# Unit 8's q and k transposed by DMA, with the kernel's whole list of work laid out anew

## The chip, the cores and the metric

The kernel runs on one core of one Trainium2 chip. A core has five engines that work from queues of their own: TensorE (in the profile PE for matmuls and PEld for weight loads), VectorE (DVE), ScalarE (ACT), GpSimd (POOL) and SyncE (SP, which here only issues transfers). Transfers run on 16 DMA engines; SyncE, ScalarE and GpSimd can issue them. The metric is the time of one execution on the device in microseconds. Before the change it is 204.08 us, the median of 3 runs (201.86 to 205.74).

## The reference, cut to what matters

Two computations follow each other: a linear attention with a decaying state, in blocks of 64 positions, for 4 batches of 8 heads, and a two-layer network with a leaky activation on its output, taken as 3072 rows of 512.

```python
B, H, S, D = 4, 8, 768, 64
for b in range(S // 64):                       # blocks of 64 positions
    qb, kb, vb = q[:, :, sl], k[:, :, sl], v[:, :, sl]
    intra = einsum('bhic,bhjc->bhij', qb, kb) * Dmask     # lam ** (i - j), 0 above the diagonal
    intra = einsum('bhij,bhjd->bhid', intra, vb)
    inter = einsum('bhid,bhde->bhie', qb * lam_pow, kv_state)
    out[:, :, sl] = intra + inter
    kv_state = lam_block * kv_state + einsum('bhsd,bhse->bhde', kb * rev_pow, vb)

x = out.transpose(0, 2, 1, 3).reshape(3072, 512)
h = x @ w_in                                   # 512 -> 2048
g = maximum(h, 0) + alpha * minimum(h, 0)
y = g @ w_out                                  # 2048 -> 512
```

## The kernel before

The attention goes by 24 units. A unit is 256 positions (two blocks of 128) of one batch and four heads: unit n is `(c, bi, hh)`, with c the chunk of the network's rows (0 to 5), bi one of its two batches and hh the half of the heads. Four units make a chunk of 512 rows, which the network then takes.

For a unit these steps are called, each a function with the unit's number:

- `load` brings q or k as float32 (tiles `qraw`, `kraw`, pools of five buffers), through SyncE's queue or, with "G", GpSimd's; `load_v16` brings v as float16 through GpSimd's.
- `cast` makes float16 of q or k into one tile `qk16`; `key_decayed` makes `kdec`, k times its decay.
- q and k must stand with the head's 64 columns on the partitions (`qkT`). Units 0 to 8 get that from TensorE: `turn` issues four 128x128 transposes for each of q and k into a PSUM bank `tp` (L316), and `turn_copy` brings them to SBUF on VectorE or ScalarE. Units 9 to 23 get it from one DMA, `turned`, on SyncE's queue (L303).
- `decayed` makes `qdT`, q times its decay. `score_products` (L377), `masked` (on VectorE, L388: `sm`), `inter` (L361) and `intra` (L402) make the output in PSUM tile `acc`, and `attended` copies it into `xT`, the network's input.
- `state_products` (L422) adds to the state in PSUM, in the other half of `acc`; `first_state` (ScalarE, L449) and `states` (VectorE, L457) bring it to `R`, which the `inter` of a later block reads. In units 4 to 7 the first block has no state before it, so `inter(n)` reads what `first_state(n)` of the same unit wrote.

The network's first layer is `up(c, f)`: four matmuls of 512 columns into a PSUM bank (L498), then `relu` on ScalarE (m, L511) and `prelu` on VectorE (g, L520). Its second layer is `down` for chunk 0 (L528, with `down_copy` and `down_store`); for chunks 1 to 5 it is `second` (L632), and the first layer of chunks 4 and 5 together is `first` (L757). These two use a scheme with seven products of half-size blocks in place of eight, which needs sums of the operands beforehand: `w_sum` of w_out, `in_sum` of w_in, `g_sum` of g and `x_sum` of xT. Each of them is one instruction on VectorE or, with "G", on GpSimd (L550 and L553).

Nothing schedules at run time. The order is a list of 1043 calls at the end of the kernel, written out by hand or by a tool, and each engine's queue holds its instructions in the order in which the calls stand there. An instruction that waits holds up all that is behind it on its engine. The engine of a step is an argument of its call ("A" ScalarE, "V" VectorE, "G" GpSimd, "P" VectorE from PSUM). PSUM banks come from a pool of four. `tick` and `fill` are matmuls whose results nobody reads, in the opening. `gate(2, "out")` is a transfer of one number of w_out on SyncE's queue: SyncE can issue none of the later loads before the third quarter of w_out has landed.

Of the kernel before, what the change touches and what calls it, by code (L numbers as in the profile page):

```python
# [11 lines left out]
def kernel(  # L12
# [16 lines left out]
    nc = tc.nc  # L29
# [452 lines left out]
    G = {}  # L482
# [299 lines left out]
    mask_logs(0)  # L782
    key_decay()
    state_decay()
    load(0, 0, "k", None)
    cast(0, "k16", "V")
    query_decay(0, 1)
    load(0, 0, "q", None)
    key_decayed(0, "V")
    mask_logs(1)  # L790
    key_decayed(1, "V")
    decay_mask(2)
    decay_mask(0)
    cast(1, "k16", "V")
    tick(56)
    load(0, 1, "q", 1, "G")
    load_v16(1)
    decay_mask(1)
    cast(1, "q16", "A")
    mask_logs(3)  # L800
    query_decay(1, 1)
    cast(0, "q16", "V")
    turn(1, (1,))
    turn_copy(1, (1,), "V")
    decay_mask(3)
    query_decay(0, 0)
    load_alpha()
    load(0, 1, "k", 1, "G")
    load_v16(0)
    turn(1, (0,))  # L810
    turn_copy(1, (0,), "V")
    load_v16(2)
    turn(0, (1,))
    turn_copy(0, (1,), "V")
    turn(0, (0,))
    turn_copy(0, (0,), "A")
    load_v16(3)
    load_win(1)
    slopes_turn()
    slopes()  # L820
    load_win(0)
    decayed(1, "P")
    cast(2, "q16", "A")
    score_products(1)
    masked(1)
    fill(3)
    key_decayed(2)
    cast(2, "k16", "A")
    cast(3, "q16", "G")
    turn(2, (0,))  # L830
    turn_copy(2, (0,), "V")
    state_in(1, 0)
    first_state(1)
    decayed(2)
    cast(3, "k16", "A")
    decayed(0)
    score_products(0)
    masked(0)
    turn(2, (1,))
    turn_copy(2, (1,), "A")  # L840
    key_decayed(3)
    inter(1)
    intra(1)
    attended(1, "A")
    load_win(3)
    turn(3, (0,))
    turn_copy(3, (0,), "A")
    state_in(0, 0)
    first_state(0)
    load(1, 0, "q", 0, "G")  # L850
    score_products(2)
    masked(2)
    turn(3, (1,))
    turn_copy(3, (1,), "A")
    state_in(2, 0)
    first_state(2)
    decayed(3)
    load(1, 0, "k", 0, "G")
    load(1, 0, "q", 1, "G")
    load_win(2)  # L860
    inter(0)
    intra(0)
    attended(0, "A")
    load_v16(4)
    load(1, 0, "k", 1, "G")
    state_in(1, 1)
    states(1, (1,))
    load_wout(0)
    score_products(3)
    masked(3)  # L870
    state_in(3, 0)
    first_state(3)
    inter(2)
    intra(2)
    attended(2, "A")
    load(1, 1, "q", 1, "G")
    state_in(2, 1)
    states(2, (1,))
    state_in(3, 1)
    states(3, (1,))  # L880
    state_in(0, 1)
    states(0, (1,))
    cast(4, "q16", "G")
    inter(3)
    intra(3)
    attended(3, "A")
    up(0, 4, 0)
    relu(0, 4, 0)
    up(0, 5)
    up(0, 3)  # L890
    up(0, 6)
    prelu(0, 4, 0)
    relu(0, 5)
    relu(0, 3)
    prelu(0, 5)
    up(0, 7)
    relu(0, 6)
    up(0, 13)
    prelu(0, 3)
    up(0, 15)  # L900
    relu(0, 7)
    prelu(0, 6)
    relu(0, 13)
    turn(4, (0,))
    relu(0, 15)
    prelu(0, 7)
    up(0, 14)
    load(1, 1, "k", 1, "G")
    prelu(0, 13)
    turn_copy(4, (0,), "A")  # L910
    up(0, 1)
    relu(0, 14)
    prelu(0, 15)
    cast(4, "k16", "G")
    turn(4, (1,))
    load_v16(5)
    load_wout(1)
    up(0, 0)
    prelu(0, 14)
    cast(5, "q16", "A")  # L920
    up(0, 4, 1)
    turn_copy(4, (1,), "A")
    relu(0, 1)
    relu(0, 4, 1)
    cast(5, "k16", "G")
    load(1, 1, "q", 0, "G")
    up(0, 9)
    key_decayed(4, "V")
    state_products(4, None, True)
    in_sum(1, 1, "G")  # L930
    score_products(4)
    load_wout(2)
    prelu(0, 1)
    prelu(0, 4, 1)
    relu(0, 0)
    relu(0, 9)
    turn(5, (0,))
    cast(7, "q16", "G")
    up(0, 12)
    relu(0, 12)  # L940
    first_state(4)
    load_wout(3)
    prelu(0, 0)
    w_sum(1, 1, "G")
    decayed(4)
    up(0, 2)
    turn_copy(5, (0,), "V")
    relu(0, 2)
    turn(5, (1,))
    prelu(0, 9)  # L950
    up(0, 11)
    relu(0, 11)
    prelu(0, 12)
    prelu(0, 2)
    key_decayed(5)
    turn_copy(5, (1,), "V")
    up(0, 8)
    gate(2, "out")
    prelu(0, 11)
    load(1, 1, "k", 0)  # L960
    relu(0, 8)
    up(0, 10)
    prelu(0, 8)
    down(0, 2, 0)
    down(0, 0, 0)
    states(4, (1,))
    inter(4)
    masked(4)
    relu(0, 10)
    down(0, 3, 0)  # L970
    intra(4)
    score_products(5)
    cast(6, "q16", "A")
    cast(7, "k16", "G")
    decayed(5)
# [873 lines left out]
```

## Time and profile before

| | us |
|---|---|
| median of 3 runs | 204.08 |
| lowest and highest run | 201.86 and 205.74 |
| the profiled execution's own time | 205.24 |
| its span, first to last instruction | 203.5 |
| mean granted TensorE clock over the span | 0.989 |

The span is the part that the trace shows; the profiled execution's own time has 1.74 us more around it. A page of the profile gives busy time by engine, 40 slices of the span, the DMA queues, the chain of work that ended last and the costliest groups of instructions. In a row of a timeline the columns are start and length in us, engine, line, operation, what is written and read, and in brackets how long the engine had been idle and what ended that. These are the slices of the page, 5.1 us each; a digit is the busy share in tenths, and PEclk is the clock that TensorE was granted:

```profile
PE   7999999995999999999999999999999999999992
DVE  6988789998989999899999998889989999995800
ACT  5895774426587699687777769455596987533022
POOL 8999859794495948999999979970386222656700
PEclk9999999998899999999999999999999999999999
DMA  5999999999949998999999953230040001103143
```

The tenth slice has the only low digit of PE between the opening and the end, and in it and the next the granted clock is lower.

### The profile page before, as it was taken

The page shows a single profiled execution, that of the slowest core. Times are in us where ns is not written, and L with a number is a line of the kernel's source. Part 1 is how long each engine was busy: PE and PEld are TensorE (multiplying, and loading weights), DVE is VectorE, ACT ScalarE, POOL GpSimd, SP SyncE. Part 2 cuts the span into 40 slices and gives each one's busy share as a digit, 9 for nine tenths or more (in the row PEclk, how much of TensorE's full clock was granted, in tenths as well). Part 3 has the DMA queues.
Part 4 walks back from the last instruction along what each step waited for, and adds up shares of the span by engine and source line. Part 5 has one row for each costly group of instructions (what it writes and reads, how often), then busy time and mean ns, then how long its engine had stood idle before and what let it go on. Part 6 is the DMA issues. An engine that isn't in the chain of part 4 may idle for free.

```text
span 203.5 us, 5865 instructions
## 1 busy us (share of the span) xinstructions
PE 195.1 (96%) x2351; PEld 129.9 (64%) x2351; DVE 175.3 (86%) x320; ACT 130.9 (64%) x281; POOL 143.6 (71%) x161
## 2 busy tenths in 40 slices
PE   7999999995999999999999999999999999999992
PEld 7775454544544498766565768766665656788892
DVE  6988789998989999899999998889989999995800
ACT  5895774426587699687777769455596987533022
POOL 8999859794495948999999979970386222656700
PEclk9999999998899999999999999999999999999999
DMA  5999999999949998999999953230040001103143
GB/s 163 280 196 228 242 269 231 199 291 224 229 52 180 278 239 236 205 223 168 196 293 169 132 77 80 78 106 0 0 156 3 0 2 52 55 19 138 45 152 116
DMA packets 59199, 30.53 MB, mean 150 GB/s; under 512 B 29652, under 2 KB 57956, under 8 KB 59172
## 3 DMA queue, kind: packets, MB, share of 16 engines
q1 hardware_dynamic: 41236, 19.87, 40.1%
q0 software_dynamic: 17776, 10.23, 35.7%
q8 instruction: 18, 0.29, 0.6%
q14 instruction: 9, 0.07, 0.1%
q10 hardware_dynamic: 160, 0.07, 0.1%
HBM read 27.27 MB, written 6.29 MB: 165 GB/s over the span
## 4 chain that ended last, share of the span: by engine, by line
PE 80%; DVE 6%; DMA 4%; POOL 4%; issue 2%; ACT 1%; DVEq 0%; POOLq 0%; ACTq 0%
PE h_ps L498 26%; PE y L632 16%; PE b L632 12%; PE b L757 5%; DMA w_in_sb<-in_moe_w_in_dram 4%; PE o_ps L528 4%; PE e L757 3%; PE a L757 3%; PE acc L402 3%; PE s L377 3%; PE acc L361 2%; POOL v L272 2%; PE acc L422 1%; DVE sm L388 1%; PE tp L316 1%
## 5 line engine op out<-in xcount | busy, mean ns | idle before, releaser
L498 PE MATMUL h_ps<-xT,w_in_sb 128*128 128x512 f16 (+1 forms) x264 | 59.6, 373 | 0.2 <-DMA w_in_sb<-in_moe_w_in_dram 0.2
L632 PEld LDWEIGHTS <-g 128*128 128x128 f16 x464 | 44.7, 98 | 10.1 <-DVE g L550 0.6
L520 DVE SCALAR_TENSOR_TENSOR g<-m,oma,h_ps 128x512 f16<-128x512 f32 (+1 forms) x66 | 46.0, 727 | 3.9 <-ACT m L511 2.8
L511 ACT ACTIVATE m<-h_ps 128x512 f32<-128x512 f32 (+1 forms) x66 | 37.4, 582 | 15.8 <-PE h_ps L498 14.8
L498 PEld LDWEIGHTS <-w_in_sb 128*128 128x128 f16 x264 | 24.4, 98 | 25.5 <-DMA w_in_sb<-in_moe_w_in_dram 1.1
L388 DVE TENSOR_TENSOR sm<-s,dmask 128x1024 f16<-128x1024 f32 x24 | 29.3, 1219 | 2.2 <-PE s L377 2.2
L632 PE MATMUL y<-w_out_sb,g 128*128 128x256 f16 x224 | 27.9, 273 | 0.3 <-DVE g L550 0.3
L550 POOL TENSOR_TENSOR g<-g 128x512 f16<-128x512 f16 x11 | 13.2, 1204 | 16.4 <-DVE s L553 16.3
L341 POOL TENSOR_TENSOR qdT<-qkT,qdecay 128x512 f16<-128x512 f16 (+1 forms) x20 | 21.0, 1056 | 4.7 <-ACT qkT L247 2.6
L632 PE MATMUL b<-t,g 128*128 128x256 f16 x160 | 19.8, 273 | 0.0
L247 ACT ACTIVATE xT<-acc 128x512 f16<-128x512 f32 x22 | 13.1, 595 | 9.6 <-PE acc L422 5.6
L272 POOL DMA_DIRECT2D v<-in_v_dram x24 | 18.8, 789 | 0.0
L457 DVE SCALAR_TENSOR_TENSOR R<-R,rdecay,acc 128x128 f16<-128x128 f16 x54 | 15.6, 342 | 2.8 <-ACT xT L247 2.2
L550 POOL TENSOR_TENSOR g<-g,g 128x512 f16<-128x512 f16 x12 | 14.3, 1204 | 5.0 <-DVE g L550 2.9
L553 POOL TENSOR_TENSOR s<-g,g 128x512 f16<-128x512 f16 x9 | 10.4, 1155 | 8.4 <-DVE g L520 8.4
L528 PE MATMUL o_ps<-w_out_sb,g 128*128 128x512 f16 x64 | 16.1, 395 | 0.0
L247 ACT ACTIVATE o_sb<-y 128x512 f32<-128x512 f32 (+2 forms) x12 | 6.2, 526 | 13.1 <-PE y L674 7.1
L290 ACT ACTIVATE kdec<-kraw,kdecay 128x64 f16<-128x64 f32 x56 | 14.0, 343 | 0.0
L292 POOL TENSOR_TENSOR kdec<-kraw,kdecay 128x512 f16<-128x512 f32 x13 | 13.8, 1068 | 0.0
L361 PE MATMUL acc<-qdT,R 128*128 128x128 f16 x80 | 8.4, 219 | 2.2 <-DVE R L457 2.0
L377 PE MATMUL s<-qkT 64*64 64x128 f16 x384 | 10.3, 222 | 0.2
L402 PE MATMUL acc<-sm,v 64*64 64x128 f16 x384 | 10.1, 224 | 0.1
(130 smaller groups left out, 371.0 us busy)
## 6 DMA issues: line engine op xcount, KB each, us to landing
out_dram<-o_sb SPq DMA_DIRECT2D x23, 256.0 KB, 2.5
kraw<-in_k_dram SPq DMA_DIRECT2D x7, 512.0 KB, 5.8
qraw<-in_q_dram SPq DMA_DIRECT2D x6, 512.0 KB, 5.6
v<-in_v_dram POOLq DMA_DIRECT2D x24, 128.0 KB, 5.2
w_in_sb<-in_moe_w_in_dram POOLq DMA_DIRECT2D x4, 512.0 KB, 7.9
w_out_sb<-in_moe_w_out_dram POOLq DMA_DIRECT2D x4, 512.0 KB, 9.6
qraw<-in_q_dram POOLq DMA_DIRECT2D x6, 256.0 KB, 7.1
qraw<-in_q_dram SPq DMA_DIRECT2D x6, 256.0 KB, 5.6
```

What stands on the lines that cost most here:

```text
L247: nc.scalar.activation(out, in_, AF.Copy)
L272: nc.gpsimd.dma_start(out=v16.rearrange("p h e d -> p h (e d)"), in_=v[2 * (c % 2) + bi, ds(4 * hh, 4), ds((c // 2) * W, W), :].rearrange( ...
L341: engine(eng).tensor_tensor(out=qdT[:, :, :, p], in0=(t["qps"] if eng == "P" else t["qkT"][:, 0])[:, :, :, p], in1=qdecay[:, hh, :, :, p], ...
L377: nc.tensor.matmul(t["s"][ds(a * 64, 64), hl, hp, 1 - e, :].rearrange("p (e j) -> p e j", e=2), lhsT=t["qkT"][p, 1, e, hp, ds(a * 64, 64)] ...
L388: nc.vector.tensor_tensor(out=t["sm"].rearrange("p a h x j -> p (a h) x j"), in0=t["s"].rearrange("p a h x j -> p (a h) x j"), in1=mask_of ...
L498: nc.tensor.matmul(h[:, 0:n] if bi is None else h[:, 0:n].rearrange("p (e j) -> p e j", e=2), lhsT=w_in_sb[:, gi, ts(f, 128)], rhs=x.rearr ...
L511: nc.scalar.activation(m[:, 0:n], HP[c, f, bi][:, 0:n], AF.Relu, scale=-1.0)
L520: nc.vector.scalar_tensor_tensor(out=g, in0=m, scalar=oma[:, f : f + 1], in1=h, op0=ALU.mult, op1=ALU.add)
L528: nc.tensor.matmul(O[c, t], lhsT=g_of(c, f)[:, t // 2, t % 2, :], rhs=w_out_sb[:, f, :], start=(f == 0), stop=(f == NF - 1),)
L550: engine(eng).tensor_tensor(out=out, in0=a, in1=b, op=ALU.subtract)
L632: nc.tensor.matmul(Y[c, k][:, ds(b * HALF, HALF)], lhsT=left(c, i, f, b), rhs=right(i, f), start=(f == 0 and b == 0 and i in (1, 5)), stop ...
L757: nc.tensor.matmul(t, lhsT=w, rhs=x, start=(g == 0 and i in (1, 5)), stop=(g == 1), skip_group_check=True)
```

## The change

Unit 8 goes over from `turn` and `turn_copy` to `turned`: eight transposes on TensorE and a copy on ScalarE are replaced by one DMA transpose on SyncE's queue. The list of calls, 1042 now, stands in another order from end to end, and some 80 steps have another engine. `prelu` takes an engine too, which no call uses. All else is computed as before.

```diff
-    turn(8, (0, 1))
-    turn_copy(8, (0, 1), "A")
+    turned(8)
...
-    def prelu(c, f, bi=None):
+    def prelu(c, f, eng="V"):
+        prelu_of(c, f, None, eng)
+
+    def prelu_half(c, f, bi):
+        prelu_of(c, f, bi, "V")
+
+    def prelu_of(c, f, bi, eng):
         g, m, h = g_of(c, f), M[c, f, bi], HP[c, f, bi]
...
-        nc.vector.scalar_tensor_tensor(
+        engine(eng).scalar_tensor_tensor(
             out=g, in0=m, scalar=oma[:, f : f + 1], in1=h, op0=ALU.mult, op1=ALU.add
         )
...
-    attended(5, "V")
+    attended(5, "A")
...
-    key_decayed(6)
+    key_decayed(6, "V")
...
-    cast(1, "k16", "V")
+    cast(1, "k16", "A")
...
-    key_decayed(1, "V")
+    key_decayed(1, "A")
...
-    cast(4, "q16", "G")
+    cast(4, "q16", "A")
```

In the opening, GpSimd's queue issues the loads of k and q of unit 2 and 3 and of v of units 0 to 3 in another order, all still ahead of the first quarter of w_in. A load of unit 4's q now stands between the first and the second quarter of w_in, where before the second followed at once.

VectorE around unit 7, before. The rows run from the masked scores of unit 5 to those of unit 7; t are sums of w_out, xT is `attended(5)`, the R behind it `states(7)`:

```order
L388 TENSOR_TENSOR sm<-s,dmask 128x1024
L550 TENSOR_TENSOR t_963<-w_out_sb,t_818 128x512
L550 TENSOR_TENSOR t_1001<-w_out_sb,t_963 128x512
L292 TENSOR_TENSOR kdec<-kraw,kdecay 128x512
L341 TENSOR_TENSOR qdT<-qkT,qdecay 128x4x64 x2
L550 TENSOR_TENSOR t_818<-w_out_sb 128x512
L249 CAST xT<-acc 128x2x4x64
L457 SCALAR_TENSOR_TENSOR R_1_2_119<-R_1_1_118,rdecay,acc 128x128 x2
L388 TENSOR_TENSOR sm<-s,dmask 128x1024
```

And now, from the masked scores of unit 5 over those of unit 7 to those of unit 6 and its state:

```order
L388 TENSOR_TENSOR sm<-s,dmask 128x1024
L292 TENSOR_TENSOR kdec<-kraw,kdecay 128x512
L249 COPY qkT<-tp 128x512
L457 SCALAR_TENSOR_TENSOR R_1_2_113<-R_1_1_112,rdecay,acc 128x128 x2
L556 TENSOR_TENSOR t_787<-w_out_sb 128x512 x2
L556 TENSOR_TENSOR t_1009<-w_out_sb,t_787 128x512
L292 TENSOR_TENSOR kdec<-kraw,kdecay 128x512
L388 TENSOR_TENSOR sm<-s,dmask 128x1024
L457 SCALAR_TENSOR_TENSOR R_1_2_119<-R_1_1_118,rdecay,acc 128x128 x2
L249 COPY qkT<-tp 128x512
L388 TENSOR_TENSOR sm<-s,dmask 128x1024
L457 SCALAR_TENSOR_TENSOR R_0_2_116<-R_0_1_115,rdecay,kv 128x128 x2
```

The xT is gone from VectorE, the two `qdT` went to GpSimd, and a second kdec, `key_decayed(6)`, stands ahead of unit 7's masked scores. Behind these rows come one sum of w_out and `cast(8, "q16", "V")`.

GpSimd in the same place, now; t and w_out_sb are sums of w_out, the cast is of unit 9's k, the kdec are of units 8 and 11:

```order
L341 TENSOR_TENSOR qdT<-qkT,qdecay 128x4x64
L251 CAST qk_1085<-kraw 128x512
L556 TENSOR_TENSOR t_1009<-w_out_sb,t_787 128x512
L556 TENSOR_TENSOR t_1093<-w_out_sb,t_1009 128x512
L292 TENSOR_TENSOR kdec<-kraw,kdecay 128x512
L556 TENSOR_TENSOR w_out_sb<-w_out_sb 128x2x256
L292 TENSOR_TENSOR kdec<-kraw,kdecay 128x512
```

Before, one v load, the cast of unit 6's k and two kdec stood there, and then two more casts. Two of the three sums shown were VectorE's.

SyncE's queue from the gate on, before and now; kraw and qraw are loads, o_sb are stores, and the transposes are those of units 9 and 10 before and of units 8 and 9 now:

```order
L115 DMA gates_123<-w_out_sb 1x1
L89 DMA kraw<-in_k_dram 128x4x128 x2
L89 DMA qraw<-in_q_dram 128x8x128
L89 DMA kraw<-in_k_dram 128x8x128
L89 DMA kraw<-in_k_dram 128x4x128
L89 DMA qraw<-in_q_dram 128x4x128
L544 DMA out_dram<-o_sb 128x512
L89 DMA kraw<-in_k_dram 128x4x128
L89 DMA kraw<-in_k_dram 128x8x128
L89 DMA qraw<-in_q_dram 128x4x128
L303 DMA_TRANSPOSE qkT<-qk_1152 128x8x128
L303 DMA_TRANSPOSE qkT<-qk_1111 128x8x128
```

```order
L115 DMA gates_123<-w_out_sb 1x1
L89 DMA kraw<-in_k_dram 128x4x128 x3
L89 DMA qraw<-in_q_dram 128x8x128
L89 DMA kraw<-in_k_dram 128x8x128
L550 DMA out_dram<-o_sb 128x512
L89 DMA kraw<-in_k_dram 128x4x128
L89 DMA qraw<-in_q_dram 128x4x128
L303 DMA_TRANSPOSE qkT<-qk_1204 128x8x128
L303 DMA_TRANSPOSE qkT<-qk_1085 128x8x128
L89 DMA kraw<-in_k_dram 128x8x128
```

A k load of half a batch and a q load went behind the first transposes, a k load of a whole batch too.

More of the change, by code (lines that the diff above doesn't have):

```diff
@@ L848 @@
[L848 to L855, printed above, removed]
-    first_state(2)
+    turn(0, (0,))
+    turn(2, (1,))
+    masked(1)
+    cast(3, "q16", "G")
+    first_state(1)
+    cast(2, "q16", "G")
+    turn_copy(0, (0,), "A")
+    turn(3, (0,))
+    inter(1)
+    turn(2, (0,))
+    load_alpha()
+    score_products(0)
+    load_win(0)
+    intra(1)
+    key_decayed(2)
+    decay_mask(0)
@@ L1222 @@
+    key_decayed(17, "A")
+    load_v16(15)
+    state_products(12)
+    second(1, 3, 1)
+    attended(11, "A")
+    second_out(1, 3)
+    masked(12)
     load(4, 0, "q", 1)
[L1223 to L1225 removed]
+    states(12, (0, 1))
     turned(13)
[L1227 to L1237 removed]
```

1664 lines of the change are left out of this document (825 added, 839 removed).

## The prediction

> **What bounds the kernel now.** I read the page's busy line first, then the busy times by stretch, then the chain of work in order of time where a stretch stands out, then the timelines of the engines in it.
>
> ```profile
> PE 195.1 (96%) x2351; PEld 129.9 (64%) x2351; DVE 175.3 (86%) x320; ACT 130.9 (64%) x281; POOL 143.6 (71%) x161
> core 0: us, PE busy (x) PEld busy (x) DVE busy (x) ACT busy (x) POOL busy (x), PEclk, DMA share, GB/s
> 0.00:18.88 18.88, 16.77 (x339) 13.38 (x340) 16.19 (x43) 13.78 (x32) 18.01 (x33) 1.00 1.12 212
> 18.88:45.00 26.12, 26.12 (x265) 13.32 (x266) 22.84 (x35) 14.17 (x27) 21.48 (x27) 1.00 1.24 247
> 45.00:55.00 10.00, 7.94 (x135) 4.92 (x134) 9.06 (x17) 4.95 (x11) 4.53 (x7) 0.83 1.09 250
> 55.00:134.00 79.00, 78.90 (x1109) 51.07 (x1108) 72.98 (x134) 60.47 (x144) 71.20 (x73) 1.00 1.01 173
> 134.00:140.00 6.00, 5.67 (x56) 3.67 (x55) 5.82 (x12) 3.28 (x6) 2.42 (x3) 1.00 0.10 34
> 140.00:199.50 59.50, 59.50 (x455) 43.55 (x452) 48.43 (x83) 33.70 (x63) 25.99 (x22) 1.00 0.15 53
> ```
>
> TensorE is the bound: from 18.88 to 45, from 55 to 134 and from 140 to 199.5 it is never idle for more than 0.1 us in all. A new order can't shorten those 164.6 us except by giving TensorE less to do. What can be won lies in the opening (to 18.88), in 45 to 55 (2.06 us idle, and a mean granted clock of 0.83) and, for 0.33 us, in 134 to 140. The chain through the bad stretch:
>
> ```profile
> 43.48 0.53 DVE t L550
> 44.00 2.43 issue
> 46.44 0.69 DVE xT L249
> 47.15 0.39 ACT R L449
> 47.56 0.62 DVE R L457 x2
> 48.22 0.27 PE acc L361 x2
> ...
> 52.54 0.45 PE tp L316 x8
> ...
> 47.15 0.38 ACT L449 ACTIVATE R<-acc 128x256 f16<-128x256 f32 x1 [3.07 <-DVE xT L249]
> ```
>
> `attended(5, "V")` (xT) stands on VectorE behind `w_sum(1, 0)` (t). ScalarE's `first_state(7)` (R, L449), which reads the same PSUM tile, waits 3.07 us for that xT with all of its queue behind it; VectorE's `states(7)` follows, and `inter(7)` on TensorE waits 2.0 us for that. Why the t at 43.40 takes so long is seen beside GpSimd's rows. The columns are start, length, engine.
>
> ```profile
> 43.40 3.11 DVE L550 TENSOR_TENSOR t<-w_out_sb 128x512 f16<-128x512 f16 x1
> 54.23 1.40 DVE L550 TENSOR_TENSOR t<-w_out_sb,t 128x512 f16<-128x512 f16 x1
> ...
> 43.59 0.62 POOL L251 CAST qk<-kraw 128x512 f16<-128x512 f32 x1
> 44.17 2.05 POOL L292 TENSOR_TENSOR kdec<-kraw,kdecay 128x512 f16<-128x512 f32 x2
> 54.19 1.16 POOL L341 TENSOR_TENSOR qdT<-qkT,qdecay 128x512 f16<-128x512 f16 x1 [2.58 <-ACT qkT L247]
> ...
> PE acc L361 <- DVE R L457: 2.0, 1, 2.0
> L550 DVE TENSOR_TENSOR t<-w_out_sb,t x6: 411/421/1400, 40.4 to 82.4; 128x512 f16<-128x512 f16 x6
> ```
>
> The same sum takes 0.42 us at the median. The one at 43.40 ends at 46.51, just after three GpSimd instructions in a row end at 46.22; the one at 54.23 ends at 55.63, just after one GpSimd instruction ends at 55.35. So a VectorE sum of two SBUF operands can be shut out while GpSimd works. [...]
>
> **The change, part by part.** The sum is made against the profiled execution, 205.24 us (span 203.5 and 1.74 around it). That lies 1.16 above the median of 204.08, and the lowest run is 201.86, so something like the stall above may well be missing in some executions.
>
> 1. *The stall at 45 to 55.* `attended(5)` moves to ScalarE, `w_sum(1, 0)` stands ahead of `states(7)` but no longer ahead of xT, and `first_state(7)` now precedes xT. Idle 10.00 - 7.94 = 2.06, and (1 - 0.83) x 10 = 1.7 lost to the clock, 3.76 together. Bounds: 0 if another wait takes its place, -3.76 if none does. I take -3.7, as the sequence of the chain above is taken apart. What is late next there is `masked(7)`, behind `key_decayed(6, "V")`, which waits for the k of unit 6:
>
> ```profile
> 38.26 0.73 SPq L115 DMA_DIRECT2D gates<-w_out_sb  x1
> 39.03 1.10 SPq L89 DMA_DIRECT2D kraw<-in_k_dram  x2
> ...
> DMA to landing us min/median/max: 4.1/5.8/7.1
> ```
>
> SyncE's first k load still follows the gate, so it lands from 39.0 + 4.1 = 43.1 on; 0.68 for kdec and 1.22 for masked give 45.0. TensorE needs it at `intra(7)`, which I place at 46.8 (below): 1.8 us in hand.
>
> 2. *Unit 8's transposes.* Off TensorE: eight, 0.45 us in the chain row at 52.54 (at a part-time half clock), and 8 x 0.056 = 0.45 by the four-in-0.22 groups elsewhere in that chain. -0.45. ScalarE loses one copy of 1.0 us, covered anyway. Added: one transpose on SyncE's queue.
>
> ```profile
> L303 SPq DMA_TRANSPOSE qkT<-qk x15: 1233/1392/3947, 57.6 to 124.3; - x15
> DMA to landing us min/median/max: 3.1/5.6/8.5
> 53.09 1.02 ACT L247 ACTIVATE qkT<-tp 128x1024 f16<-128x1024 f16 x1 [2.17 <-PE tp L316]
> 56.33 1.89 PE L498 MATMUL h_ps<-xT,w_in_sb 128*128 128x512 f16 x8
> ```
>
> Behind it in that queue stand `turned(9)` and loads for units 10 and later; each is put back by 1.39 at most, and `turned(9)` keeps its place. The new wait is `score_products(8)`'s: all that follows on TensorE is queued behind it, unit 8's masked and inter with it. When is it due? `up(1, 14)` began at 56.33. With -3.7, -0.45, +0.4 (part 3) and -0.23 for `score_products(8)`, which now comes later, it begins at 52.35. Five ups (4.56, the row at 18.88 below) and then `score_products(8)`: due at 56.9. It is fed by `cast(8, "q16", "V")`, behind `masked(6)`. `score_products(6)` ends some 5.0 of TensorE work ahead of 52.35 (three downs 2.6, half an up 0.43, one down 0.87, inter, intra and states 1.1), at 47.4. Then 1.22 masked, 0.6 R, 0.42 w_sum, 0.42 cast: 50.1. Landing 5.6 later is 55.7 (1.2 in hand), 8.5 later 58.6 (1.7 late). +0.3 taken, from 0 to +1.7, nearer the median landing.
>
> 3. *The opening.* Its loads on GpSimd's queue are the same set ahead of the first quarter of w_in, in another order, so that quarter lands no later; a q load of unit 4 now stands between the first and the second.
>
> ```profile
> 9.99 1.22 DVE L388 TENSOR_TENSOR sm<-s,dmask 128x1024 f16<-128x1024 f32 x1
> 17.21 1.47 PE L498 MATMUL h_ps<-xT,w_in_sb 128*128 128x256 f16 x8
> 17.32 0.60 ACT L247 ACTIVATE xT<-acc 128x512 f16<-128x512 f32 x1 [0.74 <-PE acc L402]
> 18.88 4.56 PE L498 MATMUL h_ps<-xT,w_in_sb 128*128 128x512 f16 x20 [0.20 <-DMA w_in_sb<-in_moe_w_in_dram]
> 54.99 2.01 ACT L290 ACTIVATE kdec<-kraw,kdecay 128x64 f16<-128x64 f32 x8
> DMA to landing us min/median/max: 7.2/7.9/9.1
> ```
>
> ScalarE now has unit 1's kdec (2.01) ahead of unit 1's q copy, and VectorE a cast of q0 ahead of the first masked. Walked through with these lengths, the first masked begins at about 10.4, not 9.99, and the fourth some 0.7 late. Then ScalarE puts `cast(4, "q16")` (0.6) between xT of unit 2 and xT of unit 3, after a load issued near 9.7 that lands near 17.2 (9.7 + 7.2 = 16.9 at the earliest, + 9.1 = 18.8 at the latest, by w_in's own landings in that queue). So `up(0, 5)` starts at 18.65 and ends at 19.5 where it ended before the wait to 18.88; `turn(4, (0,))`, 0.22, is then already done. +0.4, from -0.5 (the idle 2.1 us of the opening are there to be won) to +1.6 (the late landing).
>
> 4. *Engines and order of the rest.* Over the whole list VectorE gives about 3 us of work to GpSimd and ScalarE, which have it free (86%, against 71% and 64%). In 55 to 134 TensorE was never the one that waited: 0, from -0.1 (its idle time there) to +2 (one long block as at 43.40, less some slack). The tail after the last `first` has the same products in another order: 0.
>
> Sum: -3.7 - 0.45 + 0.3 + 0.4 = -3.45; 205.24 - 3.45 = 201.8.
>
> **The rivals.**
>
> *A, the block moves to `key_decayed(6, "V")` (slower).* At 43.1 VectorE starts it, both operands in SBUF, and GpSimd has six in a row: a cast, two w_sums, a kdec, a w_sum, a kdec: 0.62 + 3 x 1.16 + 2.05 = 6.15. If it is shut out of them all, as at 43.40, masked(7) ends at 45.0 + 6.15 = 51.2 against 46.8: 4.4 idle, and the clock's 1.7 as in 45 to 55: 201.8 + 6.1 = 207.9. It costs from a block of 1.8 us on, and turns the gain into a loss from about 3.6. For it: the row at 43.40. Against it: every other long sum in the trace got in after one instruction. [...]
>
> *B, unit 8's transpose lands late.* At 8.5 it is 1.7 late, and with an idle gap near 2 us the clock drops too, as at 48: 201.8 - 0.3 + 1.7 + 1.7 = 204.9. For it: the queues are loaded there (DMA share 1.09). [...]
>
> *C, the opening is won too.* Its idle 2.1 and the stall both go, and nothing is late: 201.8 - 0.4 - 0.3 - 1.5 = 199.6.
>
> *D, another wait takes the place of the stall,* in 55 to 134 where VectorE has 92% of the time and TensorE now arrives earlier: 201.8 + 2 = 203.8.
>
> **How the numbers follow.** The forecast 0.48, A 0.10, B 0.13, C 0.17, D 0.12. The forecast's own range is 200.6 to 203.0. 199.4 to 205.2 takes in B, C and D and leaves out most of A and the low edge of C. About 2% (4.1 us) is what a measurement of this kernel tells from no change: faster is below 200.0, most of C and a little of the forecast, 0.2; slower is above 208.2, half of A and what I haven't seen, 0.08; the rest 0.72.
>
> **What would show it.** In the changed profile: no VectorE sum over 2 us between 40 and 50 and a granted clock of 1.00 there (step 1); `score_products(8)` with no wait on SyncE's transpose (step 2); the continuous ups starting at 18.5 to 19.0 (step 3). Wrong it would be by a wait of TensorE for sm near 47 (A), for qkT near 57 (B), or by waits of more than 1 us after that (D).

## The result: slower, by three waits of one kind

| | before | changed |
|---|---|---|
| median, us | 204.19 (4 runs, 201.86 to 205.74) | 213.18 (4 runs, 210.47 to 215.89) |
| profiled execution, us | 205.24 | 215.08 |
| its span, us | 203.5 | 213.3 |
| mean granted clock | 0.989 | 0.976 |

The ratio is 1.038, with a 95% interval of 1.026 to 1.050: slower, where 201.8 (199.4 to 205.2) had been predicted. Executions of one kernel differ by 4 to 5 us here; the ratio compares the quicker ones of each kernel alone, and both profiled executions lie near the upper end of theirs, so the two traces can be set side by side.

The page of the changed kernel: busy time, two rows of its 40 slices (5.3 us each), and the engines' shares of the chain that ended last (the chain of work followed back from the last instruction):

```profile
PE 198.0 (93%) x2343; PEld 131.9 (62%) x2343; DVE 184.5 (86%) x311; ACT 132.7 (62%) x290; POOL 151.5 (71%) x167
...
PE   7889999995999998969999993999999999999993
...
PEclk9996999997899999999999999799999999999999
...
PE 61%; DVE 30%; ACT 4%; issue 2%; ACTq 0%; DVEq 0%
```

VectorE has nine instructions fewer and is busy 9.2 us longer. Its share of the chain was 6% and is 30%. Between the opening and the end PE has three low digits, in the 10th, 18th and 25th slice, in place of one, and PEclk is low in the opening and the 26th slice too, besides the 10th. The busy times by stretch of the changed kernel; the columns are busy us with the number of instructions by engine, and the granted clock:

```profile
core 0: us, PE busy (x) PEld busy (x) DVE busy (x) ACT busy (x) POOL busy (x), PEclk, DMA share, GB/s
0.00:20.00 20.00, 16.90 (x323) 14.10 (x327) 16.20 (x41) 14.13 (x36) 19.09 (x33) 0.92 1.12 219
45.00:55.00 10.00, 7.75 (x130) 4.56 (x129) 8.41 (x13) 4.01 (x9) 2.90 (x4) 0.83 0.80 197
...
80.00:95.00 15.00, 12.09 (x225) 9.24 (x223) 14.90 (x24) 9.87 (x29) 14.51 (x17) 1.00 1.35 211
95.00:130.00 35.00, 34.62 (x483) 21.36 (x481) 33.88 (x57) 28.05 (x65) 29.98 (x32) 1.00 1.05 164
130.00:140.00 10.00, 7.14 (x113) 5.01 (x114) 8.08 (x11) 2.05 (x4) 7.73 (x8) 0.83 0.44 105
```

And three of these of the kernel before:

```profile
0.00:20.00 20.00, 17.89 (x345) 13.91 (x346) 16.84 (x44) 14.21 (x32) 19.13 (x34) 1.00 1.12 214
...
80.00:95.00 15.00, 14.90 (x235) 10.19 (x233) 13.98 (x29) 11.54 (x30) 14.98 (x17) 1.00 1.50 219
...
130.00:140.00 10.00, 9.67 (x120) 6.46 (x118) 8.84 (x17) 4.17 (x8) 5.89 (x6) 1.00 0.17 56
```

TensorE's loss by stretch, idle time and clock together: the opening 17.89 - 16.90 = 1.0 and 0.08 x 20 = 1.6; 45 to 55 nothing against before, for the stall that was to go is still there (2.25 idle, 0.83); 80 to 95 2.8; 95 to 130 0.4; 130 to 140 2.5 and 0.17 x 10 = 1.7. That is 10.0; less the 0.45 of unit 8's transposes it leaves 9.6 of the 9.8 by which the span grew. The chain through two of the three waits:

```profile
43.92 4.41 DVE t L556 x2
...
50.50 0.53 DVE R L457 x2
...
127.12 5.07 DVE g L556 x2
```

Each time a pair of VectorE sums stands in it with over 4 us, where a pair takes 0.8. The rows of VectorE, TensorE and GpSimd at the first and the third wait; L272 is GpSimd issuing a transfer, the load of a v:

```profile
43.84 4.47 DVE L556 TENSOR_TENSOR t<-w_out_sb 128x512 f16<-128x512 f16 x2
51.16 0.37 PE L361 MATMUL acc<-qdT,R 128*128 128x128 f16 x2 [2.25 <-DVE R L457]
86.12 4.35 DVE L556 TENSOR_TENSOR t<-w_out_sb,t 128x512 f16<-128x512 f16 x2
92.69 0.38 PE L361 MATMUL acc<-qdT,R 128*128 128x128 f16 x4 [2.34 <-DVE R L457]
127.04 5.15 DVE L556 TENSOR_TENSOR g<-g,g 128x512 f16<-128x512 f16 x2
132.86 0.55 PE L361 MATMUL acc<-qdT,R 128*128 128x128 f16 x4 [3.24 <-DVE R L457]
...
42.44 0.78 POOL L272 DMA_DIRECT2D v<-in_v_dram  x1
43.24 0.69 POOL L341 TENSOR_TENSOR qdT<-qkT,qdecay 128x256 f16<-128x256 f16 x1
43.86 0.61 POOL L251 CAST qk<-kraw 128x512 f16<-128x512 f32 x1
44.43 2.25 POOL L556 TENSOR_TENSOR t<-w_out_sb,t 128x512 f16<-128x512 f16 x2
46.65 1.04 POOL L292 TENSOR_TENSOR kdec<-kraw,kdecay 128x512 f16<-128x512 f32 x1
...
127.70 0.80 POOL L272 DMA_DIRECT2D v<-in_v_dram  x1
128.53 2.27 POOL L556 TENSOR_TENSOR g<-g,g 128x512 f16<-128x512 f16 x2
130.75 1.15 POOL L341 TENSOR_TENSOR qdT<-qkT,qdecay 128x512 f16<-128x512 f16 x1
```

GpSimd's rows follow each other without a gap from 42.44 to 46.65 + 1.04 = 47.69, and from 126.60 to 130.75 + 1.15 = 131.90. VectorE's sums come free some 0.3 us later, the long one of the first pair at 47.97 and the second pair at 127.04 + 5.15 = 132.19. In each of the two runs stands the issue of a v load.

### The profile page after: what moved, and what is told of

It reads as the page before. It is cut to its first block, busy times and chain, and to the rows that moved or that the text cites. A ratio compares the mean times of both kernels' runs of the same rounds, so it can differ in the third digit from the quotient of the medians.

```text
span 213.3 us, 5867 instructions
## 1 busy us (share of the span) xinstructions
PE 198.0 (93%) x2343; PEld 131.9 (62%) x2343; DVE 184.5 (86%) x311; ACT 132.7 (62%) x290; POOL 151.5 (71%) x167
## 4 chain that ended last, share of the span: by engine, by line
PE 61%; DVE 30%; ACT 4%; issue 2%; ACTq 0%; DVEq 0%
PE h_ps L498 16%; PE b L638 10%; PE y L638 10%; DVE g L526 7%; DVE sm L388 7%; DVE g L556 5%; PE b L763 5%; DVE t L556 4%; DVE R L457 4%; PE a L763 3%; PE e L763 3%; PE acc L402 3%; PE unread L145 2%; PE o_ps L534 2%; PE s L377 2%
## 5 line engine op out<-in xcount | busy, mean ns | idle before, releaser
L498 PE MATMUL h_ps<-xT,w_in_sb 128*128 128x512 f16 (+1 forms) x264 | 60.7, 379 | 0.1
L526 DVE SCALAR_TENSOR_TENSOR g<-m,oma,h_ps 128x512 f16<-128x512 f32 x66 | 45.0, 725 | 2.5 <-ACT m L511 2.3
L247 ACT ACTIVATE xT<-acc 128x512 f16<-128x512 f32 x24 | 14.3, 596 | 21.2 <-PE acc L422 10.1
L341 POOL TENSOR_TENSOR qdT<-qkT,qdecay 128x512 f16<-128x512 f16 (+1 forms) x21 | 22.1, 1052 | 6.7 <-DMA qkT<-qk 5.8
L559 POOL TENSOR_TENSOR s<-g,g 128x512 f16<-128x512 f16 x12 | 14.3, 1195 | 10.7 <-PE b L763 4.6
L272 POOL DMA_DIRECT2D v<-in_v_dram x24 | 18.7, 782 | 0.1
L290 ACT ACTIVATE kdec<-kraw,kdecay 128x64 f16<-128x64 f32 x64 | 16.1, 337 | 0.0
L556 POOL TENSOR_TENSOR g<-g,g 128x512 f16<-128x512 f16 x11 | 12.9, 1194 | 2.2 <-DVE g L556 2.2
L556 POOL TENSOR_TENSOR g<-s,g 128x512 f16<-128x512 f16 x7 | 8.2, 1185 | 8.2 <-DVE g L556 6.7
L361 PEld LDWEIGHTS <-R 128*128 128x128 f16 x80 | 6.3, 100 | 12.3 <-issue 9.0
L402 PE MATMUL acc<-sm,v 64*64 64x128 f16 x384 | 10.9, 234 | 0.6 <-DVE sm L388 0.6
```

Of the source, the lines that this page charges most:

```text
L247: nc.scalar.activation(out, in_, AF.Copy)
L272: nc.gpsimd.dma_start(out=v16.rearrange("p h e d -> p h (e d)"), in_=v[2 * (c % 2) + bi, ds(4 * hh, 4), ds((c // 2) * W, W), :].rearrange( ...
L341: engine(eng).tensor_tensor(out=qdT[:, :, :, p], in0=(t["qps"] if eng == "P" else t["qkT"][:, 0])[:, :, :, p], in1=qdecay[:, hh, :, :, p], ...
L498: nc.tensor.matmul(h[:, 0:n] if bi is None else h[:, 0:n].rearrange("p (e j) -> p e j", e=2), lhsT=w_in_sb[:, gi, ts(f, 128)], rhs=x.rearr ...
L526: engine(eng).scalar_tensor_tensor(out=g, in0=m, scalar=oma[:, f : f + 1], in1=h, op0=ALU.mult, op1=ALU.add)
L556: engine(eng).tensor_tensor(out=out, in0=a, in1=b, op=ALU.subtract)
```

## The experiments

The expectations name theories by letters. L: a VectorE sum with both operands in SBUF is shut out for as long as GpSimd works without a gap. S: for one GpSimd instruction only. M: taking one such stall away only moves the wait. U: unit 8's transposes and the queues cost the time. P, F and B: it depends on the moment at which VectorE asks, on the forms of the instructions, or on the load by other engines. D: it is the issue of a transfer in GpSimd's unbroken run that does it. O: the opening's order and loads cost the time. The number in square brackets is the median of the kernel before on the same chip.

**The victims moved, one stall at a time (a_s1, a_s2, a_s3, a_s123).** Each of the first three takes the sums of one stall out of GpSimd's run, later on VectorE or over to GpSimd itself; a_s123 does all of it.

```diff
a_s1
-    w_sum(1, 2)
...
-    w_sum(1, 0)
...
-    w_sum(2, 0)
...
-    key_decayed(6, "V")
...
+    key_decayed(6, "V")
...
-    w_sum(3, 0)
...
+    w_sum(1, 2)
+    w_sum(1, 0)
+    w_sum(2, 0)
+    w_sum(3, 0)
a_s2
+    w_sum(4, 2, "G")
+    w_sum(4, 0, "G")
...
-    w_sum(4, 2)
-    w_sum(4, 0)
a_s3
-    g_sum(2, 4, 0, 1)
...
-    g_sum(2, 4, 0, 0)
...
+    g_sum(2, 4, 0, 1, "G")
+    g_sum(2, 4, 0, 0, "G")
```

> The changed kernel with the first wait's sums moved: w_sum(1, 2), w_sum(1, 0), w_sum(2, 0) and key_decayed(6) stand on VectorE behind masked(7) and states(7) instead of ahead of them. Theory L (a VectorE sum of two SBUF operands is shut out for as long as GpSimd runs without a gap, and what stands behind it on VectorE makes TensorE wait): inter(7) waits under 0.5 us instead of 2.4, no half-clock stretch at 51 to 54, span shorter by 2.4 to 4.1 us, about 1.02 to 1.03 of before; the waits at 92 and 132 stay. Theory U (unit 8's transposes by DMA and what they push back in the queues cost the time): as the changed kernel, 1.04 of before, TensorE waits near 50 all the same, for data.

> The changed kernel with w_sum(4, 2) and w_sum(4, 0) given from VectorE to GpSimd, ahead of decayed(11). Theory L: masked(12) is no longer held up by them, inter(12) waits under 0.5 us instead of 2.5, span shorter by 2 to 2.5 us (no half-clock stretch belonged to it), about 1.026 of before; the waits at 51 and 132 stay. Theory U: 1.04, the wait at 92 stays.

> The changed kernel with g_sum(2, 4, 0, 1) and g_sum(2, 4, 0, 0) given from VectorE to GpSimd, behind decayed(21). Theory L: states(20) follows masked(20) at once, inter(20) waits under 0.5 us instead of 3.4, no half-clock stretch at 133 to 136, span shorter by 3.4 to 5.1 us, about 1.013 to 1.022 of before; the waits at 51 and 92 stay. Theory U: 1.04, the wait at 133 stays.

> All three moves at once. Theory L: the three waits and the half-clock stretches behind them go, shorter by 8.3 (waits alone) to 11.7 us (with two stretches of 1.7): 0.98 to 1.00 of before. Theory U: 1.03 to 1.04 of before.

Measured: 216.41, 214.25, 219.39 and 215.67 us [204.61]. Each wait for the moved sums went from its place, and none of it came back as time. In a_s1 TensorE had no idle time from 45 to 55, but then waited 4.03 us ahead of 91.77 and 3.23 ahead of 134.51. In a_s2 the waits were 1.91 at 77.8 and 3.26 at 129.6. In a_s3 and a_s123 `inter` at the third place still waited 1.67 us, now for a qdT of GpSimd, and the next sum in line, `in_sum(2, 1)`, took 7.6 us. The timeline of a_s123 there:

```profile
131.59 7.62 DVE L556 TENSOR_TENSOR s<-s,w_in_sb 128x512 f16<-128x512 f16 x1
...
123.57 0.81 POOL L272 DMA_DIRECT2D v<-in_v_dram  x1
...
137.78 1.14 POOL L556 TENSOR_TENSOR x<-xT 128x512 f16<-128x512 f16 x1
...
139.92 3.57 PE L498 MATMUL h_ps<-xT,w_in_sb 128*128 128x512 f16 x8 [4.32 <-DVE g L526]
```

GpSimd has no gap from 121.34 to 138.92, with the one issue at 123.57 in it; VectorE gets in at 138.92 + 0.29. So it was shown that a sum can be shut out for many instructions (S can't give 7.6 us), and M too: a victim taken away leaves the next one, and the more is given to GpSimd, the longer its run. The v load issued at 123.57 had landed at 128.27, before the sum was asked for, so it isn't the transfer itself that shuts the sum out.

The waits also come and go between executions. In a_s2's trace TensorE has no wait at 48 and in a_s3's none at 90, though nothing was moved there. In a_s2 GpSimd had a gap of 0.62 us ahead of 43.76, waiting for the k of its cast, and the pair of sums beside it took 0.75 us; in a_s3 the pair at 86.43 took 2.45, each of them let in next to a further issue.

**The same in the kernel before (b_s1).** There the sum that was shut out at 43.40 was moved behind unit 7.

```diff
-    w_sum(1, 0)
...
+    w_sum(1, 0)
```

> The kernel before with w_sum(1, 0) moved from ahead of attended(5) on VectorE to ahead of w_sum(3, 0), about eight us later. Theory L: the long sum at 43.40 is gone from in front of xT of unit 5, inter(7) waits under 0.5 us instead of 2.0 to 2.2, no half-clock stretch near 49, 2 to 4 us shorter: 0.98 to 0.99 of before. Rival M (the wait only moves: the sum, or another, is shut out where it now stands, and TensorE waits there as long): 0.99 to 1.01.

204.93 us [205.49]: no change. In the trace the stall at 48 was gone, with no loss of clock there; the sum that now stood at 58.96 took 2.56, and TensorE waited up to 0.8 at a time from 57 to 65. M holds there as well.

**More victims away, and GpSimd relieved (a_s1234, a_relief).** a_s1234 adds two sums to a_s123; a_relief then gives eleven casts of GpSimd to ScalarE.

```diff
a_s1234
-    in_sum(2, 1)
+    in_sum(2, 1, "G")
...
-    in_sum(4, 1)
+    in_sum(4, 1, "G")
a_relief
-    cast(15, "k16", "G")
+    cast(15, "k16", "A")
... 
```

> The three moves, and in_sum(2, 1) and in_sum(4, 1) given from VectorE to GpSimd as well: in_sum(2, 1) is the sum that took 7.62 us beside six GpSimd instructions when only the three moves were made. Theory L: no VectorE sum over 2.5 us, TensorE's waits of 1.8 and 4.5 us near 135 to 140 and the half-clock stretch of 6.8 us behind them go, 6 to 9 us shorter than with the three moves: 0.99 to 1.02 of before. Rival M: another sum is shut out as long a little later, 1.05 to 1.07.

> As the one before, and eleven casts of q or k given from GpSimd to ScalarE (0.62 us each, 6.8 us of GpSimd's work between 85 and 130). Theory L: GpSimd's unbroken run ends earlier and what still waits for it waits less: 0 to 3 us shorter than without the casts. Rival (ScalarE, 62% busy, then holds up TensorE's PSUM banks): 0 to 3 us longer, with waits of TensorE for ScalarE.

210.50 and 210.53 us [205.49]. In both, the next VectorE sum, an `x_sum`, took 4.26 and 4.25 us. It cost TensorE less there: its longest wait behind it was 0.88 us in a_s1234, where that of a_s123 was 4.32, and the median fell by 5.2 us. So moving a sum does pay where little hangs on the next one. Eleven instructions fewer on GpSimd brought nothing: its busy time isn't what decides here.

**What shuts VectorE out, by itself (p_lock, p_lock2, p_lock3).** Three programs that set VectorE's sums beside rows of GpSimd instructions. In a string, t is a GpSimd sum, D the issue of a v load, g a sum that waits for ScalarE and so leaves a gap of 0.7 us ahead of it; the second number is the casts from PSUM that VectorE does before it asks for its sum.

```diff
p_lock
+        block(4, g_sums, lambda: v_sum(0))
+        block(6, g_sums, lambda: v_sum(0), lambda: v_sum(1))
+        block(4, g_sums, v_psum)
...
p_lock3
+        block("tttttttt", 4, [0])
+        block("tDtttttt", 4, [0])
+        block("tDtttttt", 6, [0])
+        block("tttDtttt", 7, [0])
+        block("ttttDttt", 2, [0])
+        block("tDtgtttt", 7, [0])
+        block("tDtttttt", 4, ["psum"])
+        block("tDtttttt", 4, ["copy"])
+        block("tDtttttt", 4, [0, 1])
+        block("tDDttttt", 5, [0])
```

> A kernel that computes nothing of the reference: VectorE does one sum of two 128x512 f16 operands in SBUF while GpSimd does n sums of the same form, n = 0, 1, 2, 4, 6 (with 6, two VectorE sums in a row); then at n = 4 a VectorE sum with one operand in PSUM, a VectorE copy with one SBUF operand, GpSimd casts in place of sums, and GpSimd sums that each wait for ScalarE, so with gaps. Theory L (shut out until GpSimd stops): 0.42 us alone, about 1 at n = 1, 2 at n = 2, 4.4 at n = 4, 6.5 at n = 6, the second sum there 0.42; 0.4 to 0.6 with the PSUM operand; at the gaps it gets in at the first, so 1.2 at most. Theory S (the loser is blocked for one instruction): 1.2 at most at every n.

> Computes nothing of the reference: one VectorE sum of two SBUF operands against unbroken GpSimd runs of five to seven instructions, asked for at 14 moments 32 ns apart, then with mixed GpSimd forms (casts, products with f32, transfers issued), with a scalar_tensor_tensor ahead on VectorE, with operands of one tile, and with TensorE and ScalarE at work beside it. Theory P (which of the two engines gets the next turn hangs on the moment of asking): at some moments 1.1 us at most, at others shut out to the end of the run, 4 us or more. Theory F (it hangs on the forms of GpSimd's instructions): all 14 moments alike, the mixed runs long. Theory B (it hangs on load from other engines): long only in the last three.

> Computes nothing of the reference: unbroken runs of eight GpSimd instructions, sums only, or with one or two issues of a transfer (D) among them, and one VectorE sum of two SBUF operands asked for at a chosen place, each case twice. Theory D (once GpSimd has issued a transfer, it keeps the port over all that follows without a gap): without D, or with D still to come, the sum takes 1.4 us at most; asked for right behind the D of tDtttttt or two sums later, 3 to 7 us, to the end of the run; behind the D of tttDtttt 3 to 4; with a gap of GpSimd between the D and the asking, 1.4 at most; with one operand in PSUM 0.7 all the same; of two sums behind the D only the first is long. Theory P (a matter of the moment of asking alone): no difference between runs with and without D.

p_lock spoke for S: beside two to six GpSimd sums in a row one VectorE sum took 1.11 us (0.41 alone), and two took 2.40. L as stated fell. p_lock2 shifted the moment of asking in steps of 32 ns, mixed the forms and loaded the other engines: without an issue a sum never took over 1.38 us, so P, F and B fell too. One case was long, 3.92 us: VectorE asked while GpSimd issued a transfer. Another with two issues took 1.48. p_lock3 told the cases apart. Its timeline, first without D, then with D just behind the first sum, then with a D still to come when VectorE asks:

```profile
11.78 8.30 POOL L91 TENSOR_TENSOR px<-px 128x512 f16<-128x512 f16 x8 [11.33 <-DVE px L99]
14.34 0.86 DVE L69 TENSOR_TENSOR vx<-vx 128x512 f16<-128x512 f16 x1
...
21.84 0.90 POOL L93 DMA_DIRECT2D dx<-in_v_dram  x1
22.77 6.01 POOL L91 TENSOR_TENSOR px<-px 128x512 f16<-128x512 f16 x6
23.24 5.82 DVE L69 TENSOR_TENSOR vx<-vx 128x512 f16<-128x512 f16 x1
...
47.08 4.35 POOL L91 TENSOR_TENSOR px<-px 128x512 f16<-128x512 f16 x4 [0.83 <-DVE px L99]
48.12 0.42 DVE L69 TENSOR_TENSOR vx<-vx 128x512 f16<-128x512 f16 x1
51.38 0.78 POOL L93 DMA_DIRECT2D dx<-in_v_dram  x1
```

The same sum took 0.86, 5.82 and 0.42. Asked two sums later it took 4.25; with D as fourth 3.53; each of them ended just after GpSimd's last sum. With a gap between D and the asking it took 0.44, a sum with one operand in PSUM 0.68, a copy from SBUF to SBUF 5.56 (0.98 in p_lock, with no issue); of two sums behind a D the first took 5.70 and the second 0.41. With two D in a row it took 3.72 and got in ahead of GpSimd's last sum. Every case ran twice, within 0.13 of each other. S agrees with 0.86, as a GpSimd sum of that row took 8.30 / 8 = 1.04, and disagrees with 5.82: behind a D it was six instructions, 6.01 us. The port of which the expectation speaks is the author's guess: the traces show who waited and how long, and no port.

I also counted, over all nineteen traces, the boundaries between two GpSimd instructions that follow without a gap, at which such a VectorE sum (those that took more than 0.55 us) was waiting. In a run with no issue so far it got in at all 121. Behind an issue it was passed over at 135 and got in at 20, 13 of these next to a further issue. So D is the rule, with exceptions whose cause is open: at 86 in the changed kernel the sum got in behind the two kdec, ahead of the run's end, and in b_v8 sums at 51.78 and 57.88, behind an issue, took 1.39 and 0.84.

**Unit 8 alone, and the opening alone (b_u8dma, a_open4).** The kernel before with nothing changed but unit 8; and the kernel with four stalls' sums moved, with the first 111 calls of the kernel before put in.

```diff
b_u8dma
-    turn(8, (0, 1))
+    turned(8)
...
-    turn_copy(8, (0, 1), "A")
```

> The kernel before with nothing changed but unit 8's q and k transposed by DMA at the place in the list where TensorE transposed them. If that part costs nothing: 0.990 to 1.005 of before (up to 0.45 us of TensorE saved), score_products(8) waits under 0.3 us. If its landing is late: TensorE waits at score_products(8) by the transpose's landing, 1 to 3 us, 1.005 to 1.02.

> The changed kernel with the moves of sums (the three and the fourth) and, for its first 111 calls, the order and engines that the kernel before has there. If the new opening costs 2 to 3 us (later transposes of units 1 and 3, a half-clock stretch between 12 and 22): 2 to 3.5 us shorter than with the four moves alone, 1.01 to 1.015 of before, no half-clock stretch before 25. If the opening costs nothing, or GpSimd's unbroken run decides all that follows: within 1 us of the four moves alone.

b_u8dma: 205.60 us [204.95], ratio 1.013, interval 1.007 to 1.020. In the old order `score_products(8)` comes too early for the landing, which TensorE's row shows:

```profile
52.04 0.42 PE L377 MATMUL s<-qkT 64*64 64x128 f16 x16 [1.39 <-DMA qkT<-qk]
```

In the changed kernel the transfer was issued at 56.44 and landed at 61.95, and the products began at 62.67 without a wait. So U is worth some 1.3% here, and there, in the profiled execution, no wait of TensorE. a_open4 (218.32 us [204.95]) said nothing of the opening: the two halves of the list didn't fit, and unit 4's transposes waited 5.5 us at 23.4 for a cast.

**The transfer issue moved (a_v23, a_s12v, b_v8).** D says that the sums may stay where they are if the issue leaves the run. a_v23 is the changed kernel with one line moved: v of unit 23 is loaded ahead of the earlier GpSimd sums, behind which GpSimd has a gap. a_s12v has a_s1 and a_s2 besides. b_v8 is the kernel before with v of unit 8 issued ahead of its run at 43.

```diff
a_v23
+    load_v16(23)
     g_sum(2, 2, 0, 0, "G")
...
-    load_v16(23)
b_v8
     load_v16(6)
+    load_v16(8)
...
-    load_v16(8)
```

> The changed kernel with one line moved: load_v16(23), GpSimd's issue that stands ahead of two g_sums and a product in the run at 126 to 132, goes ahead of g_sum(2, 2, 0, 0), into GpSimd's idle time at 120. No instruction of VectorE, ScalarE or TensorE moves. Theory D: the g_sums of VectorE at 127 take 0.4 to 1.4 us each instead of 1.0 and 4.2, inter(20) waits under 0.8 us instead of 3.4, the half-clock stretch behind it goes, 3 to 5 us shorter; the waits at 51 and 92 stay, and in_sum(2, 1) takes 1.4 at most. Theory P: 4 us again there, or by chance not.

> The changed kernel with the first two moves of sums, and load_v16(23) moved as in the run before. Theory D: none of the three waits, and none in their place: no VectorE sum over 2.2 us after 45, 7 to 11 us shorter than the changed kernel, 0.99 to 1.015 of before. Theory P: a long sum in some other place, 1.03 or more.

> The kernel before with one line moved: load_v16(8), the GpSimd issue at 42.81 ahead of the sum of 3.11 us, goes ahead of in_sum(1, 3), behind load_v16(6). Theory D: that sum takes 1.2 us at most, inter(7) waits 0.5 us at most instead of 2.0 to 2.2, no half-clock stretch near 49; the executions all lie at 201.0 to 202.5 us where those of before lie between 201.7 and 205.9: 0.98 to 1.00 of before. Theory P: as before.

a_v23: 207.05 us [205.21], ratio 1.000, interval 0.986 to 1.014, where the changed kernel had 213.18. Its ten executions range from 202.34 to 217.74, seven below the changed kernel's lowest (210.47) and three above it, so the size of the gain isn't known closely. The place at 127, now at 124, in its timeline:

```profile
124.44 2.29 DVE L556 TENSOR_TENSOR g<-g,g 128x512 f16<-128x512 f16 x2
...
125.11 2.62 POOL L556 TENSOR_TENSOR g<-g,g 128x512 f16<-128x512 f16 x2
...
127.39 0.38 PE L361 MATMUL acc<-qdT,R 128*128 128x128 f16 x4 [0.39 <-ACT mem L247]
```

The same two sums beside the same GpSimd sums take 2.29 in place of 5.15, TensorE waits 0.39 in place of 3.24, and no clock is lost there. In that execution the sums at 44 got through as well, and the timeline shows why:

```profile
45.02 0.75 DVE L556 TENSOR_TENSOR t<-w_out_sb 128x512 f16<-128x512 f16 x2
...
45.45 0.79 POOL L251 CAST qk<-kraw 128x512 f16<-128x512 f32 x1 [0.33 <-DMA kraw<-in_k_dram]
```

The k of GpSimd's cast landed late, and the gap of 0.33 us ended the run with the issue in it. The wait at 90 stayed (2.39), as nothing was done about it. a_s12v: 207.25 us [205.21], ratio 1.018, interval 1.005 to 1.030, 206.59 to 209.49: none of the three waits in its trace. Next to a_s1 and a_s2 alone (216.41, 214.25) it points to the moved issue, which a_v23 shows alone; its median is no shorter than a_v23's, so what the moved sums add isn't shown.

b_v8: 204.96 us [205.21], ratio 0.993, interval 0.985 to 1.000. The sum at 43.52 took 0.42 in place of 3.11, TensorE didn't stall at 48, and no clock was lost. With the issue gone, GpSimd stood idle beside that sum, waiting for a k:

```profile
44.09 0.61 POOL L251 CAST qk<-kraw 128x512 f16<-128x512 f32 x1 [1.11 <-DMA kraw<-in_k_dram]
```

So this trace shows the stall gone, but doesn't tell an issue in the run from the run itself, as a_v23 and p_lock3 do. One of ten executions has a mean clock of 0.992 or less; of the kernel before, 11 of 23 lie from 0.988 to 0.992, where its profiled one with the stall has 0.989. So the stall with its loss of clock is mostly gone, and yet the executions still lie from 201.6 to 206.4, where those of the kernel before lie from 201.7 to 206.2: that stall alone isn't what parts them, as the prediction supposed, and what does is open. Two more of its twelve executions took 284.91 and 398.34 us, are left out of the ratio, and stay unexplained.

**The opening (a_open1, a_s12vo).** In the changed kernel `key_decayed(0)` and `cast(0, "q16")` on VectorE fall beside GpSimd's casts and issues from 9 to 13 us. They took 0.79 and 0.42 us in its profiled execution, but 2.22 for the first in a_v23 and 1.88 for the second in a_s1, which have the same opening. a_open1 is the changed kernel with both ahead of that, and the load of q called earlier, so it can't tell D from O alone; a_s12vo has this and a_s12v.

```diff
+    load(0, 0, "q", None)
...
+    key_decayed(0, "V")
     turn_copy(1, (1,), "V")
+    cast(0, "q16", "V")
...
-    load(0, 0, "q", None)
...
-    key_decayed(0, "V")
...
-    cast(0, "q16", "V")
```

> The changed kernel with key_decayed(0) and the cast of unit 0's q, both VectorE's, asked for ahead of turn_copy(1, (1,)) instead of beside GpSimd's run of casts and transfer issues at 10 to 13 (the two took 0.7 to 2.2 us there, whichever of them came first, in the kernels of this family); nothing else moves. Theory D: neither takes more than 0.8 us, the transposes at 12 do not wait for the cast of q (they waited 0.4 to 2.4), no half-clock stretch between 11 and 24, the 60th matmul of up comes at 30.5 to 31.3 (changed kernel 32.7, kernel before 31.0); the waits later on come and go as before, so 1.02 to 1.04 of before. Rival O (the opening is late for its order on ScalarE or its loads): the 60th still comes at 32.5 or later.

> The same two moves in the kernel with the first two moves of sums and load_v16(23) ahead. Theory D: 2 to 4 us shorter than without them, 0.995 to 1.01 of before; half clock only where TensorE idles at the end. Rival O: as without them, 1.01 to 1.03.

a_open1: 211.21 us [204.54]. The clock stayed at 1.00 from 15 to 20 (0.69 in the changed kernel), and the 60th matmul of the first layer began at 30.59 (32.71; before the change 31.01); the wait at 127 was still there, with 3.50. a_s12vo: 206.25 us [204.54], ratio 1.017, interval 1.010 to 1.024, at a mean clock of 0.997 in the profiled execution. Against a_s12v (207.25, ratio 1.018) that is 1.0 us by the medians and nothing by the ratios, where D had 2 to 4 us and O had no gain: what the opening costs is open. The stretches of a_s12vo where the changed kernel had its waits:

```profile
50.00:55.00 5.00, 5.00 (x55) 2.50 (x54) 4.97 (x10) 2.77 (x6) 3.52 (x4) 1.00 0.68 140
90.00:95.00 5.00, 5.00 (x76) 2.96 (x75) 4.94 (x9) 3.92 (x11) 4.98 (x6) 1.00 1.18 205
130.00:135.00 5.00, 5.00 (x72) 3.29 (x69) 5.00 (x9) 2.02 (x4) 5.00 (x5) 1.00 0.02 3
```

TensorE is never idle there. So 213.18 - 206.25 = 6.9 of the 9.0 us between the medians went with these four edits, and with the clock that was lost at the waits; by the ratios, 1.038 and 1.017, it is a little over half of the loss. What is left has small waits in it (1.48 at 77.0, 0.74 at 57.5, 0.57 at 79.9, 0.93 at 13.5 for a v load) which weren't tried one by one; the rest of it is open. Nor was the changed kernel with unit 8 left to TensorE tried. No version ran that beats the kernel before.

## Why the prediction was wrong, step by step

**Step 1, the stall at 45 to 55 goes: -3.7, measured 0.** This step failed. The way in which the stall held TensorE up was read rightly, and what was late next was looked for in the wrong place. I walked through `key_decayed(6)` and the landing of its k, 43.1 + 0.68 + 1.22 = 45.0 for the end of masked(7), and gave no time at all to `w_sum(1, 2)` and `w_sum(1, 0)`, which stand ahead of both. The first was shut out for 4.1 us; masked(7) ended at 49.29 + 1.22 = 50.51, and TensorE waited 2.25, for the R behind it, with 1.7 of clock. My own row at 43.40, three instructions long, had a transfer issue of GpSimd 0.6 us ahead of it, in a row that I didn't show:

```profile
42.81 0.79 POOL L272 DMA_DIRECT2D v<-in_v_dram  x1
```

I didn't ask what set it apart from the row at 54.23, which was one. Rival A had this mechanism, on the instruction next to the right one, at a chance of 0.10 because "every other long sum in the trace got in after one instruction". All of those but one (1.38 us at 36.22, let in between two issues) had no issue ahead of them in GpSimd's run: in the old order 58 of VectorE's 65 sums were asked for where GpSimd stood idle or hadn't issued anything in its run, and of the other seven only the one at 43.40 took over 1.4 us.

**Step 2, unit 8: -0.45 and +0.3.** The first stands, with eight matmuls fewer (2343 against 2351); the second, put at +0.3 in a range from 0 to +1.7, was 0. The landing took 5.5 us (61.95 - 56.44), by the median of 5.6 that was used. Rival B, which needed 8.5, didn't happen.

**Step 3, the opening: +0.4 (-0.5 to +1.6), measured 1.0 idle and 1.6 of clock.** A term mis-sized: the continuous ups began at 20.66 and not at 18.5 to 19.0, and the clock, counted for the stall at 48, wasn't counted here. The walk took VectorE's unhindered lengths. Two steps put ahead of GpSimd's run brought the 60th matmul forward by 2.1 us and the clock to 1.00 (a_open1). That is one profiled execution a side; in the changed kernel's own those two steps weren't long, so what in its opening brings the clock down is open.

**Step 4, the rest: 0 (-0.1 to +2), measured about +7.** This is the other step that failed, and the dearest. "VectorE gives about 3 us of work to GpSimd and ScalarE, which have it free" took the shares of busy time as room. GpSimd's busy time grew by 7.9 us; in runs of it that hold transfer issues two more pairs of sums were shut out, and took 4.35 and 5.15 us, and TensorE lost 2.8 and 4.2 in those stretches. The bound of +2 was "one long block as at 43.40, less some slack". It was two, besides that of step 1, and each longer, since the length is set by GpSimd's run. Rival D named the place and not the mechanism.

**The range.** The three waits have one cause and were given chances as if each stood alone. If step 1 fails for this reason, step 4 does too, at several places. A rival with steps 1 and 4 failing together, at what they measured, ends at 201.8 + 3.7 + 7.0 = 212.5; with step 2's +0.3 gone, and 2.6 in step 3 in place of 0.4, it is 214.4, against the 215.08 of the profiled execution.

## What to carry to other kernels

Where GpSimd works without a gap and issues a transfer in between, a VectorE sum or copy whose operands all lie in SBUF may wait until GpSimd stops (in p_lock3 5.82 us for a sum and 5.56 for a copy; with no issue ahead 0.86 there and 0.98 in p_lock), so look for its issues and its gaps, not for its busy share, before work is given to it or put beside it. Try to move the issue out of the run, ahead of a gap, before the sums: one moved line took away at 127 the wait that two moved sums had only passed on (0.39 us in a_v23, 4.32 at the next place in a_s3). And when one stall is longer than the others of its kind, as 3.11 us was beside 1.40, find out what sets that row apart before the forecast rests on it.

## What the runs showed of the hardware

In these runs a GpSimd transfer issue mostly shut VectorE's SBUF-to-SBUF work out for the rest of an unbroken run (5.82 us against 0.86 in p_lock3), not for an instruction. GpSimd's own sums weren't held up meanwhile: 6.01 / 6 = 1.00 us each in p_lock3, and 4.02 for four, where four beside which a VectorE sum was let in took 4.35. A copy with a single SBUF operand was shut out just so (5.56), a sum with one operand in PSUM wasn't (0.68), and a gap on GpSimd ended it (0.44 behind one of 0.74 us in p_lock3; one of 0.33 was enough in a_v23).

The granted clock fell to 0.50 for stretches of 3.41 us, or of two or three times that: in the changed kernel at 16.9, 51.0 and 132.9, in the kernel before at 49.0, for 6.8 us in a_s1, a_s3 and a_s123 (means of 0.55 from 90 to 95 in a_s1, 0.79 from 130 to 145 in a_s3, and 0.984 over the 212.6 us of a_s123), and for 10.2 in a_s12v and a_s1234 (0.66 from 10 to 25 in a_s12v, 0.973 over the 211.0 us of a_s1234). A stretch of 3.41 us costs some 1.7: in the chain of the changed kernel four matmuls of `down` take 1.67 us in one, and 0.86 behind it. The stretches came with waits of 2.25 and 3.24 us, 2.02 in the kernel before and 1.91 in a_s2, but not with those of 2.34 at 92.7 and of 2.29 in a_s3, and TensorE had no wait over 0.69 from 2 us on up to the one at 16.9. In the changed kernel's trace their starts lie whole multiples of 3.41 us apart: 34.13 and 81.92 us, ten and 24 of them. What starts a stretch, and why one wait of 2.3 us passes without one and another doesn't, isn't shown.
